# GpSimd's local attention products issued as two instructions, one for each head

## The chip, the cores and the metric

One NeuronCore of a Trainium2 chip runs the whole kernel. The metric is the device time of one execution in microseconds (us). Its compute engines, by the names of the profile, are PE (TensorE, matmuls), DVE (VectorE), ACT (ScalarE) and POOL (GpSimd); SP only issues DMAs.

## What is computed

Attention over q, k, v of shape (4, 8, 576, 64), then two pairs of dense layers on the 2304 rows of 512 that it leaves. The attention has two parts that are added: a downsampled one (mean over 4 tokens) and a local one, in which each token sees the seven tokens around it:

```python
mask = np.abs(pos[:, None] - pos[None, :]) < factor          # factor = 4
scores = np.where(mask, scale * np.matmul(q, k.transpose(0, 1, 3, 2)), -1e9)
attn = softmax(scores)
out = out_up + np.matmul(attn, v)
# then, on x = out as (2304, 512):
g = s * np.maximum(x @ w_in, 0) ** 2 + b;   x = g @ w_out
h = x @ w2_in;   out = (h - np.tanh(h)) @ w2_out
```

## The kernel before

The 2304 rows are cut into eight units of 288, u = 0 to 7. PE runs the first dense pair unit by unit (`l1`, line 741, into the tile `ph`; `l2_1`, line 774, into `acc`), each product as three matmuls on split operands (`gh` and `gl`, `wh` and `wl`). While PE works on unit u, the other engines make the attention of unit u + 1 (and begin that of u + 2), so that its x is there when PE comes to it. After unit 7 the second dense pair runs, with no attention beside it.

For units 2 to 7 the local attention is not made with matmuls. `local_items(u)` holds the two heads of a partition side by side (tiles `Q` of 128 x 2 heads x 9 tokens x 64, `K` and `V` with a window of 15 tokens) and makes, for each of NO = 7 offsets o, an elementwise product of 128 x 1152 elements:

- `mult(o, eng, kind)` makes Q times K (line 181), and `red(o)` sums it over the 64 elements into a score `s` (line 186, on DVE);
- after a softmax over the offsets (`sm1`, `sm2`), `pv(o, eng, kind)` makes V times the weight `a` (line 249), and `pvadd(o)` adds it to `O` (line 257, on DVE).

The constants `QK_POOL` and `PV_POOL` give two of the seven offsets in each part to POOL (tile `pP`); one or two of V times a go to ACT (`pA`), the rest to DVE (`pD`, `O`). So POOL makes 4 products in each of six units, 24 in all, and DVE reads each of them once. There is one buffer for each of `pP`, `pD` and `pA`: POOL's second product of a part waits until DVE has read the first. POOL also adds for the downsampled part (`raw`, line 350, and `pp`, line 351) and splits weights (`w`, line 730), and writes a column of ones into `gh` for unit 1 (line 761, a MEMSET).

`spread` puts the items of a unit into the 16 steps of the unit before by their costs (1.26 for an item of DVE, 0 for one of POOL), and a scheduler in the tile framework then orders the instructions of each engine by its own estimates, so an edit of one engine's instructions can move those of others. Each engine runs its own list in order.

Of the kernel before, what the change touches and what calls it, by code (L numbers as in the profile page):

```python
# [11 lines left out]
ALU = mybir.AluOpType  # L12
AX = mybir.AxisListType.X

B, H, S, D = 4, 8, 576, 64
# [8 lines left out]
SEG, TAU, WIN, NO = 18, 9, 15, 7  # L24
# [54 lines left out]
def attention_moe_moe_kernel(ctx: ExitStack, tc, q, k, v, w_in, w_out, s_in, b_in, w2_in, w2_out, out):  # L79
    nc = tc.nc  # L80
    pe, act, dve, pool, sp = nc.tensor, nc.scalar, nc.vector, nc.gpsimd, nc.sync
# [52 lines left out]
    Qt, Kt, Vt, Ot, X = {}, {}, {}, {}, {}  # L134
# [29 lines left out]
    def local_items(u):  # L164
# [4 lines left out]
        def ptile(shape, kind):  # L169
            t = {"O": "O", "p": "pP", "d": "pD", "a": "pA"}[kind]  # L170
            return late.tile(shape, F32, tag=t, name=t)
# [5 lines left out]
        def mult(o, eng, kind):  # L177
            def f():
                p = ptile([128, 2, TAU, D], kind)
                st[o] = p  # L180
                eng.tensor_tensor(out=p, in0=Qt[u], in1=Kt[u][:, :, o:o + TAU, :], op=ALU.mult)  # L181
            return f

        def red(o):
# [7 lines left out]
        d = [o for o in range(NO) if o not in qk_pool]  # L192
        p = list(qk_pool)
        busy, due = None, 0
        while d or p or busy is not None:
# [3 lines left out]
            elif d and due:  # L199
                o = d.pop(0)  # L200
# [6 lines left out]
            else:  # L207
                o = d.pop(0)
# [29 lines left out]
        def pv(o, eng, kind):  # L238
            def f():
                p_ = ptile([128, TAU, 2, D], kind)  # L240
                st["v", o] = p_
                if eng is act:
                    for h in range(2):
                        for t in range(TAU):
                            act.activation(out=p_[:, t, h], in_=Vt[u][:, h, o + t], func=AF.Copy,
                                           scale=st["a"][:, h * TAU + t, o:o + 1])
                    return
                aw = st["a"].rearrange("p (h t) o -> p t h o", h=2)[:, :, :, o:o + 1]
                eng.tensor_tensor(out=p_, in0=Vt[u][:, :, o:o + TAU, :].rearrange("p h t d -> p t h d"),  # L249
                                  in1=aw.to_broadcast([128, TAU, 2, D]), op=ALU.mult)  # L250
                if kind == "O":
                    Ot[u] = p_
            return f
# [6 lines left out]
        d = [o for o in range(NO) if o not in pv_pool and o not in pv_act]  # L260
# [658 lines left out]
    for s_, (n, u, i) in enumerate(seq):  # L919
# [10 lines left out]
        p_ = ps_ph.tile([128, NB1], F32, tag="ph", name="ph")  # L930
# [89 lines left out]
    for j in range(NBLK2):  # L1020
        for i in range(NF):
            p_ = ps_ph.tile([128, NB2], F32, tag="ph", name="ph2")
# [48 lines left out]
```

## Time and profile before

| | |
|---|---|
| time, median of 3 runs | 991.27 us |
| the three runs | 996.5, 991.27, 985.89 us |
| the profiled execution | 995.71 us, of which the span of the program 993.9 us |
| busy, share of the span | PE 950.1 us (96%), DVE 625.8 us (63%), ACT 473.3 us (48%), POOL 167.2 us (17%) |
| TensorE clock granted, mean | 0.961 of full speed |
| DMA | 80.85 MB, 81 GB/s on the mean |

All rows below are of that one profiled execution. A busy time counts what the profile takes as an instruction's duration, from its start to its end: an engine that has begun an instruction and is held up within it counts as busy. Idle time before an instruction stands in brackets behind a row, with what ended it. The engine that is busy 96% of the time can only be made to wait less; how much it waits is seen stage by stage.

### The profile page before, as it was taken

To read this page: it belongs to the slowest core of one execution; us is meant where nothing else is said; L and a number is where in the kernel's file an instruction comes from. 1 tells how busy PE (TensorE), PEld (TensorE's weight loads), DVE (VectorE), ACT (ScalarE), POOL (GpSimd) and SP (SyncE) were. 2 spreads that over 40 slices of the span, in tenths; PEclk is the share of its full clock that TensorE was granted. 3 is DMA by queue.
4 is the path that set the end of the run, shared out by engine and by line. 5 is a ranking of instruction groups with operands and counts; after the bars stand their busy time and mean duration, and the time that the engine had idled before them with its cause. 6 is when DMAs were issued, how large, how long until landed. Compare 5 with 4: busy or idle time off the path is not lost.

```text
span 993.9 us, 17097 instructions
## 1 busy us (share of the span) xinstructions
PE 950.1 (96%) x6554; PEld 879.4 (88%) x6554; DVE 625.8 (63%) x1102; ACT 473.3 (48%) x1352; POOL 167.2 (17%) x128
## 2 busy tenths in 40 slices
PE   8979998889989999999999999999999999999997
PEld 7868888779989989989999999999999999999996
DVE  4488898989999899796775962333333333333332
ACT  4549844436646564655586942332323232323222
POOL 1244453531613332241000000000000000000000
PEclk8559999979999999999999999999999999999999
DMA  9990053223222314120074810101001010100000
GB/s 226 303 347 1 3 198 112 77 78 130 76 83 98 96 49 134 30 64 1 25 276 179 291 46 1 43 2 43 22 22 41 3 43 1 44 1 22 1 22 21
DMA packets 59895, 80.85 MB, mean 81 GB/s; under 512 B 22454, under 2 KB 44710, under 8 KB 59814
## 3 DMA queue, kind: packets, MB, share of 16 engines
q1 hardware_dynamic: 59814, 79.76, 25.3%
q8 instruction: 51, 0.84, 0.3%
q14 instruction: 30, 0.25, 0.1%
HBM read 69.72 MB, written 10.03 MB: 80 GB/s over the span
## 4 chain that ended last, share of the span: by engine, by line
PE 57%; DVE 23%; issue 6%; DMA 6%; ACT 4%; POOL 2%; SPq 2%; DVEq 0%; POOLq 0%; ACTq 0%
PE ph L741 28%; PE acc L997 20%; PE acc L774 7%; DVE pp L353 3%; DVE O L257 3%; DVE s L186 2%; DVE pD L181 2%; DVE gl L762 2%; DVE wf L722 1%; DVE pD L249 1%; DMA K<-in_k_dram 1%; DMA wraw<-in_moe_w_in_dram 1%; DVE xq L314 1%; SPq L502 1%; DMA vraw<-in_v_dram 1%
## 5 line engine op out<-in xcount | busy, mean ns | idle before, releaser
L741 PE MATMUL ph<-xh,w 128*128 128x288 f32 x1024 | 238.3, 307 | 4.4 <-DVE gl L762 4.2
L774 PE MATMUL acc<-gh,w 128*128 128x288 f32 (+1 forms) x1024 | 230.5, 300 | 8.1 <-DVE yst L797 4.9
L741 PE MATMUL ph<-yxh,w 128*128 128x256 f32 x1152 | 228.4, 281 | 0.0
L741 PEld LDWEIGHTS ph<-yxh,w 128*128 128x128 f32 x1152 | 187.1, 189 | 6.3 <-DVE gl L985 0.2
L981 DVE TENSOR_TENSOR ph<-ph,th 128x256 f32<-128x256 f32 x144 | 62.3, 433 | 205.0 <-ACT th L980 204.9
L741 PEld LDWEIGHTS ph<-xh,w 128*128 128x128 f32 x1024 | 175.7, 193 | 11.9 <-DVE gl L762 7.3
L774 PEld LDWEIGHTS acc<-gh,w 128*128 128x128 f32 x1024 | 173.9, 191 | 11.0 <-DVE yst L797 5.9
L997 PE MATMUL acc<-w,gh 128*128 128x512 f32 x576 | 180.1, 393 | 0.0
L741 PE MATMUL ph<-yxl,w 128*128 128x256 f32 x576 | 161.9, 281 | 0.0
L741 PE MATMUL ph<-xl,w 128*128 128x288 f32 x512 | 154.7, 302 | 4.8 <-DVE xl L663 3.1
L980 ACT ACTIVATE th<-ph 128x256 f32<-128x256 f32 x144 | 55.5, 385 | 216.7 <-PE ph L741 216.7
L774 PE MATMUL acc<-gl,w 128*128 128x288 f32 x512 | 152.5, 298 | 0.3 <-DVE gl L762 0.3
L741 PEld LDWEIGHTS ph<-yxl,w 128*128 128x128 f32 x576 | 108.7, 189 | 6.2
L997 PE MATMUL acc<-w,gl 128*128 128x512 f32 x288 | 113.9, 395 | 0.0
L997 PEld LDWEIGHTS acc<-w,gh 128*128 128x128 f32 x576 | 98.6, 189 | 13.3
L741 PEld LDWEIGHTS ph<-xl,w 128*128 128x128 f32 x512 | 98.8, 193 | 6.3 <-DVE xl L663 3.5
L774 PEld LDWEIGHTS acc<-gl,w 128*128 128x128 f32 x512 | 97.6, 191 | 0.7 <-DVE gl L762 0.5
L985 DVE TENSOR_TENSOR gl<-ph,gh 128x256 fp32r<-128x256 f32 x144 | 61.0, 424 | 56.8 <-PE acc L997 29.9
L753 ACT ACTIVATE ph<-ph 128x288 f32<-128x288 f32 x128 | 51.3, 401 | 83.2 <-PE ph L741 80.6
L984 ACT CAST gh<-ph 128x256 fp32r<-128x256 f32 x144 | 53.8, 374 | 64.4 <-DVE ph L981 64.4
L762 DVE TENSOR_TENSOR gl<-ph,gh 128x288 fp32r<-128x288 f32 x128 | 57.4, 448 | 32.7 <-ACT gh L759 32.5
L997 PEld LDWEIGHTS acc<-w,gl 128*128 128x128 f32 x288 | 54.1, 188 | 12.4
(133 smaller groups left out, 1251.7 us busy)
## 6 DMA issues: line engine op xcount, KB each, us to landing
wraw<-in_moe_w_in_dram SPq DMA_DIRECT2D x32, 512.0 KB
wraw<-in_moe_w_out_dram SPq DMA_DIRECT2D x32, 512.0 KB
y<-yst SPq DMA_DIRECT2D x36, 144.0 KB
K<-in_k_dram SPq DMA_DIRECT2D x5, 960.0 KB
V<-in_v_dram SPq DMA_DIRECT2D x5, 960.0 KB
raw<-in_q_dram SPq DMA_DIRECT2D x24, 144.0 KB
raw<-in_k_dram SPq DMA_DIRECT2D x24, 144.0 KB
Q<-in_q_dram SPq DMA_DIRECT2D x6, 576.0 KB
```

Source lines behind the costliest of these rows:

```text
L181: eng.tensor_tensor(out=p, in0=Qt[u], in1=Kt[u][:, :, o:o + TAU, :], op=ALU.mult)
L257: dve.tensor_tensor(out=Ot[u], in0=Ot[u], in1=st["v", o], op=ALU.add)
L353: dve.tensor_reduce(out=t2.rearrange("p a h d -> p (a h) d").unsqueeze(3), in_=t[:GH].rearrange("p a h r d -> p (a h) d r"), axis=AX, op=A ...
L741: pe.matmul(p_, w_, x_, start=n == 0, stop=n == 3 * KC - 1)
L753: act.activation(out=p_, in_=p_, func=AF.Relu)
L762: dve.tensor_tensor(out=gl, in0=p_, in1=gh[:, :NB1].bitcast(F32), op=ALU.subtract)
L774: pe.matmul(accs[u][e][:, :g_.shape[1]], w_, g_, start=i == first and n == 0, stop=i == last and n == 2)
L980: act.activation(out=t, in_=p_, func=AF.Tanh)
L981: dve.tensor_tensor(out=p_, in0=p_, in1=t, op=ALU.subtract)
L984: act.copy(out=gh, in_=p_)
L985: dve.tensor_tensor(out=gl, in0=p_, in1=gh.bitcast(F32), op=ALU.subtract)
L997: pe.matmul(accs[j][t], g_, w_, start=i == 0 and n == 0, stop=i == NF - 1 and n == 2)
```

## The change

Where the engine is POOL, each of the two products is issued as two instructions, one for each head, over half of the same tiles. DVE and ACT keep theirs.

```diff
         def mult(o, eng, kind):
             def f():
                 p = ptile([128, 2, TAU, D], kind)
                 st[o] = p
-                eng.tensor_tensor(out=p, in0=Qt[u], in1=Kt[u][:, :, o:o + TAU, :], op=ALU.mult)
+
+                for h in ([slice(0, 1), slice(1, 2)] if eng is pool else [slice(0, 2)]):
+                    eng.tensor_tensor(out=p[:, h], in0=Qt[u][:, h], in1=Kt[u][:, h, o:o + TAU, :], op=ALU.mult)
             return f
...
-                eng.tensor_tensor(out=p_, in0=Vt[u][:, :, o:o + TAU, :].rearrange("p h t d -> p t h d"),
-                                  in1=aw.to_broadcast([128, TAU, 2, D]), op=ALU.mult)
+                vw = Vt[u][:, :, o:o + TAU, :].rearrange("p h t d -> p t h d")
+                aw = aw.to_broadcast([128, TAU, 2, D])
+                for h in ([slice(0, 1), slice(1, 2)] if eng is pool else [slice(0, 2)]):
+                    eng.tensor_tensor(out=p_[:, :, h], in0=vw[:, :, h], in1=aw[:, :, h], op=ALU.mult)
```

The change has four more lines than the kernel before, so its lines carry other numbers: 181 becomes 183, 186 becomes 188, 249 becomes 254, 257 becomes 261, 350 and 351 become 354 and 355, 761 becomes 765, 762 becomes 766 and 797 becomes 801.

In most of the 24 places POOL's list now has two rows where it had one, next to each other, and the second of them waits for nothing. Here is the list at the first product of unit 2, before and after (what an instruction waits for stands in brackets, as counters of engines and of DMA queues):

```order
L730 TENSOR_TENSOR w<-wf,w 128x512 [waits DMAHW6_49,Activation_49]
L761 MEMSET gh 128x2 [waits PE_49]
L181 TENSOR_TENSOR pP<-Q,K 128x1152 [waits DMAHW5_49,DMAHW4_49]
L761 MEMSET gh 128x2 [waits DVE_49,PE_49]
L181 TENSOR_TENSOR pP<-Q,K 128x1152 [waits DVE_49]
L350 TENSOR_TENSOR raw_1701<-raw_1701 72x4x128 [waits DMAHW2_49,DMAHW7_49,DMAHW1_49,DMAHW0_49]
```

And the same place of the change:

```order
L734 TENSOR_TENSOR w<-wf,w 128x512 [waits DMAHW6_49,Activation_49]
L765 MEMSET gh 128x2 [waits PE_49]
L183 TENSOR_TENSOR pP<-Q,K 128x576 [waits DMAHW5_49,DMAHW4_49]
L765 MEMSET gh 128x2 [waits DVE_49,PE_49]
L183 TENSOR_TENSOR pP<-Q,K 128x576
L183 TENSOR_TENSOR pP<-Q,K 128x576 [waits DVE_49]
L183 TENSOR_TENSOR pP<-Q,K 128x576
L354 TENSOR_TENSOR raw_1701<-raw_1701 72x4x128 [waits DMAHW2_49,DMAHW7_49,DMAHW1_49,DMAHW0_49]
```

The second product has become two rows in a row; of the first, the second half stands behind a MEMSET that waits for DVE and PE.

On DVE the scheduler has moved one instruction. This is DVE's list where PE has begun unit 5 and the last result of unit 4 is taken out of `acc` into `yst`; before:

```order
L353 TENSOR_REDUCE pp2_5188<-raw72_5090 72x256
L257 TENSOR_TENSOR O_5413<-O_5413,pA_5394 128x1152
L797 TENSOR_SCALAR yst_5041<-acc_4304,scal_86,bcol_87 128x288
L762 TENSOR_TENSOR gl_5068<-ph_5052,gh_5067 128x288
L257 TENSOR_TENSOR O_5413<-O_5413,pP_5535 128x1152
L181 TENSOR_TENSOR pD_5754<-Q_5322,K_5324 128x1152
L762 TENSOR_TENSOR gl_5114<-ph_5098,gh_5113 128x288
```

And the same place of the change:

```order
L357 TENSOR_REDUCE pp2_5206<-raw72_5107 72x256
L261 TENSOR_TENSOR O_5432<-O_5432,pA_5413 128x1152
L183 TENSOR_TENSOR pD_5775<-Q_5340,K_5342 128x1152
L801 TENSOR_SCALAR yst_5058<-acc_4317,scal_86,bcol_87 128x288
L766 TENSOR_TENSOR gl_5085<-ph_5069,gh_5084 128x288
L261 TENSOR_TENSOR O_5432<-O_5432,pP_5554 128x1152
L766 TENSOR_TENSOR gl_5131<-ph_5115,gh_5130 128x288
```

The product `pD` (of unit 7) has gone up by three rows, ahead of `yst`. On PE one group of three matmuls, on ACT one of the small `pA` instructions and on SP one store of y stand some rows elsewhere at the same place; everything else keeps its order.

## Rows read from the trace of the kernel before

**Rows 1.** Busy us (x instructions) of each engine by stretch, granted PE clock, DMA.

```profile
core 0: us, PE busy (x) PEld busy (x) DVE busy (x) ACT busy (x) POOL busy (x), PEclk, DMA share, GB/s
130.00:490.00 360.00, 333.16 (x2490) 315.98 (x2489) 324.55 (x456) 196.44 (x658) 118.62 (x64) 0.97 0.26 83
490.00:994.00 504.00, 497.57 (x3278) 458.12 (x3276) 208.80 (x457) 190.30 (x468) 0.00 (x0) 1.00 0.17 55
...
200.00:250.00 50.00, 43.68 (x313) 41.95 (x312) 45.60 (x71) 25.68 (x82) 11.52 (x6) 0.90 0.33 103
```

**Rows 2.** Chain of work that ended last: shares of the span by engine.

```profile
PE 57%; DVE 23%; issue 6%; DMA 6%; ACT 4%; POOL 2%; SPq 2%; DVEq 0%; POOLq 0%; ACTq 0%
```

**Rows 3.** Instructions by line: count, duration ns min/median/max, first and last start us.

```profile
L181 DVE TENSOR_TENSOR pD<-Q,K x30: 1324/1349/4227, 133.4 to 448.1; 128x1152 f32<-128x1152 f32 x30
L181 POOL TENSOR_TENSOR pP<-Q,K x12: 2609/2676/6080, 133.4 to 440.1; 128x1152 f32<-128x1152 f32 x12
...
L249 POOL TENSOR_TENSOR pP<-V,a x12: 2151/2720/3361, 172.1 to 479.6; 128x1152 f32<-128x1152 f32 x12
...
L730 POOL TENSOR_TENSOR w<-wf,w x24: 1266/1354/2158, 42.6 to 128.2; 128x512 fp32r<-128x512 f32 x24
```

**Rows 4.** DVE timeline, long instructions: start us, duration us, engine, line, operation, tiles.

```profile
139.32 3.30 DVE L181 TENSOR_TENSOR pD<-Q,K 128x1152 f32<-128x1152 f32 x1
...
173.29 3.31 DVE L249 TENSOR_TENSOR pD<-V,a 128x1152 f32<-128x1152 f32 x1
...
208.69 3.04 DVE L415 TENSOR_SCALAR E<-E,zz 72x144 f32<-72x144 f32 x4
...
269.75 2.27 DVE L410 TENSOR_SCALAR zz<-zz 72x4 f32<-72x4 f32 x1
...
430.24 4.23 DVE L181 TENSOR_TENSOR pD<-Q,K 128x1152 f32<-128x1152 f32 x1
...
480.26 2.68 DVE L257 TENSOR_TENSOR O<-O,pA 128x1152 f32<-128x1152 f32 x1
```

**Rows 5.** DVE timeline, instructions of the same kinds that were not held up.

```profile
193.75 0.48 DVE L415 TENSOR_SCALAR E<-E,zz 72x144 f32<-72x144 f32 x2
...
434.39 1.34 DVE L257 TENSOR_TENSOR O<-O,pA 128x1152 f32<-128x1152 f32 x1
...
436.03 0.15 DVE L410 TENSOR_SCALAR zz<-zz 72x4 f32<-72x4 f32 x1
```

**Rows 6.** POOL timeline, instructions back to back while DVE is held up.

```profile
50.68 2.49 POOL L730 TENSOR_TENSOR w<-wf,w 128x512 fp32r<-128x512 f32 x2
...
138.75 2.65 POOL L181 TENSOR_TENSOR pP<-Q,K 128x1152 f32<-128x1152 f32 x1 [1.43 <-DVE s L186]
141.37 2.40 POOL L350 TENSOR_TENSOR raw<-raw 72x512 f32<-72x512 f32 x1
...
429.33 1.30 POOL L350 TENSOR_TENSOR raw<-raw 72x512 f32<-72x512 f32 x1 [4.50 <-DMA y<-yst]
430.58 2.67 POOL L181 TENSOR_TENSOR pP<-Q,K 128x1152 f32<-128x1152 f32 x1
```

**Rows 7.** DVE timeline: one held up by POOL before 130 us, and one reduce.

```profile
50.39 3.33 DVE L722 SCALAR_TENSOR_TENSOR wf<-wraw 128x512 int32<-128x512 int32 x1
...
142.91 1.34 DVE L186 TENSOR_REDUCE s<-pD 128x18 f32<-128x1152 f32 x1
```

**Rows 8.** POOL's product and DVE's read of it, where DVE waits for it.

```profile
440.09 3.65 POOL L181 TENSOR_TENSOR pP<-Q,K 128x1152 f32<-128x1152 f32 x1 [6.36 <-DVE s L186]
...
443.78 1.35 DVE L186 TENSOR_REDUCE s<-pP 128x18 f32<-128x1152 f32 x1 [0.94 <-POOL pP L181]
```

**Rows 9.** PE timeline: three waits for DVE, with idle us and releaser.

```profile
211.27 0.30 PE L427 MATMUL PT<-ident,E 72*72 72x72 f32 x1 [4.59 <-DVE E L415]
...
424.79 0.40 PE L774 MATMUL acc<-gh,w 128*128 128x288 f32 x1 [1.03 <-DVE yst L797]
...
436.16 0.40 PE L741 MATMUL ph<-xh,w 128*128 128x288 f32 x1 [1.09 <-DVE gl L762]
```

## The prediction

> **What bounds the kernel now.** I read the busy time by stretch first. From 490 us on, PE is busy 497.57 of 504 us and POOL does nothing [rows 1]: no edit of POOL can shorten that half. The change acts from 130 to 490 us, where all of POOL's local products lie [rows 3]. There PE is busy 333.16 of 360 us and DVE 324.55, both about nine tenths: neither alone is the bound. PE works in order and waits, in short pieces, for DVE instructions that stand behind others in DVE's list [rows 9]. PE's idle time there, 360 - 333.16 = 26.8 us, is the most that faster work of DVE could give back, beside what the clock takes: it was granted at 0.97 of full speed on the mean there, and at 0.90 from 200 to 250 us. The chain of waits says the same in one line: PE 57%, DVE 23%, POOL 2% [rows 2]. POOL's own speed hardly matters; what it does to DVE does.
>
> It does something. A DVE product of 128 x 1152 takes 1.35 us on the median, but the longest 4.23 [rows 3]. The long ones stand in the timeline beside a POOL instruction: DVE's product at 139.32 took 3.30 us, and POOL's at 138.75 ended at 141.40, which is 1.2 us before DVE's end [rows 4, 6]. So DVE stood still until POOL was done, and then did its work. Ten DVE instructions between 130 and 490 us are held up by one of the 24 products, the first at 139.32 and the last at 480.26; six stand in rows 4 and their unhindered durations in rows 3 and 5. By each one's duration less the unhindered one, the ten lose 20.2 us together (1.95 at 139.32, 2.9 at 430.24, 1.3 at 480.26). Only DVE instructions with two inputs in SBUF are among them, and small TENSOR_SCALARs (zz, 2.27 us in place of 0.15); a reduce beside POOL keeps its 1.34 us [rows 4, 5, 7].
>
> **What the change does to this.** It removes no work: 24 POOL instructions become 48 of half the size.
>
> The price of a half: no half stands in the trace. The nearest row is POOL's 128x512 product, 1.27 us at least, against 2.61 for 128x1152 [rows 3]: 2.1 ns for each element and 0.19 us fixed, which makes 1.40 for 576 elements. Two back to back overlap by 0.05 us (2.49 for two of 1.27 [rows 6]), so a pair takes 2.75 us, 0.14 more than one. For V times a, 2.15 at least, I take the same 0.14. Bounds: nothing more at all, and twice the 0.19, that is 0.38. All 24 cost POOL 24 x 0.14 = 3.4 us, which its idle time hides: it is busy 118.62 of 360 us [rows 1].
>
> What matters is who goes next when the first half ends while DVE stands waiting. The trace shows both. At 141.40 POOL had its next instruction ready and DVE got in: POOL's sum `raw` took 2.40 us, waiting in its turn [rows 6]. But at 430.24 DVE waited while `raw` ran to 430.63, POOL's product followed at 430.58 and ran its plain 2.67 us, and DVE came after both, 4.23 us in all [rows 4, 6]. At 50.39 two equal products of POOL followed each other from 50.68 to 53.17 in 2.49 us, and DVE waited for both, 3.33 us in all [rows 6, 7]. That last case is the one nearest to two halves: same operation, same partitions, nothing to wait for in between. I take it: the pair stays glued, DVE waits as long as before and 0.14 more.
>
> The Trainium skill (SBUF — State Buffer, section "Who interferes with whom") says that whoever issues first "gets the shared pair for the whole instruction; the other fully blocks". The held-up rows above agree with it (3.30 against 1.35 us). Read to the letter it would let DVE in between two halves and speak for the change; that is the first rival below. The Trainium skill's GPSIMD Engine Reference (section "Instruction dispatch") says that POOL's cores start the next instruction as soon as each has finished its share of the one before, which speaks against it; the overlap of 0.05 us agrees.
>
> The sum if glued: 10 stalls x 0.14 = 1.4 us. Then DVE's reads of `pP` that already wait for POOL or come within 0.3 us of its end, like the one at 443.78 that idled 0.94 us [rows 8]: five, 5 x 0.14 = 0.7. Then the moved `pD`: `yst` now stands behind 1.35 us of it, and PE already waited 1.03 us for that `yst` at 424.79. PE starts 1.35 later there, but 11 us on it idled 1.09 us for DVE anyway, at 436.16 [rows 9], and DVE has no more to do than before; 0.3 is left (bounds 0 and 1.35). Behind the MEMSET that has come between the first product's halves stands POOL's second half and nothing urgent but DVE's read; the MEMSET had no idle time of its own before, so I take 0 (bound 1.4, if PE frees its buffer late). Sum +2.4 us, taking each us of DVE as one of the end, which is the upper price.
>
> The sum if DVE gets in every time: now what follows DVE's held-up instruction counts, since POOL's second half goes after it. A reduce or the short `gl`, in three of the ten, runs beside it: at 139.32, 173.29 and 269.75 DVE saves about half a product, 1.2 + 1.0 + 0.9 = 3.1 us. In the seven others the next instruction needs the same way in: at 430.24 an `O` sum follows [rows 5], and at 208.69 three more of the four TENSOR_SCALARs. It meets the second half, waits for the rest, and the 0.14 is lost: 7 x 0.14 = 1.0. Net -3.1 + 1.0 + 0.7 + 0.3 = -1.1 us. Either way it is at most a quarter of one per cent.
>
> The profiled execution took 995.71 us, 4.4 above the median of 991.27; the three runs lie 10.6 us apart. The forecast against its own time is 995.71 + 2.4 = 998.1, against the median 991.27 + 2.4 = 993.7. I forecast no change, at 993.7 us; its own range, from DVE let in every time (990.2) to the upper bounds of every term (10 + 5 times 0.38, 1.35, 1.4: +8.5), is 990 to 1000.
>
> **The rivals.**
>
> *Faster: every stall is halved.* If DVE gets in between the halves and keeps the way in for its next instruction too, ten stalls of 20.2 us become 10.1. Of this the end sees what PE waited for. The best case is at 211.27, where PE had idled 4.59 us for the `E` of rows 4 and the clock of that stretch was 0.90 [rows 1, 9]: at full clock all through, 50 x 0.10 = 5 us come back on top. 991.27 - 10.1 = 981.2, and 976 with the clock. For it: the handover at 141.40. Against it: the two cases at 50.39 and 430.24, and that seven of ten followers collide. It decides only if nearly all of the 10.1 us reach PE.
>
> *Slower: the read of `pP` comes late.* POOL now has to get in twice. If DVE lets each second half wait for one more of its products (1.35 us), POOL's result is 1.5 us late, and DVE, which reads it in the order of its list, idles; five products of the twelve of Q times K have less than that to spare (like the one in rows 8), 5 x 1.5 = 7.5 us, and with the moved `pD` (1.35) and the MEMSET (1.4) it is 10.3: 1001.5 us. A new fall of the clock to half speed would come on top. It decides once the five lose more than about 1.4 us each. Against it: between 441 and 444 us DVE runs a reduce, and this does not compete.
>
> *It does nothing at all that can be seen* is the forecast's own middle; it needs no other mechanism.
>
> **How the numbers follow.** About 1% is what a measurement of this kernel can tell from no change, since its runs lie that far apart. The forecast, glued or let in, has 0.74; the faster rival 0.13, the slower 0.13. Each rival ends at about 1% from 991.27, and the faster and slower chances are theirs: 0.13, 0.74, 0.13. The range goes from 984 (a good part of the faster rival's way, and the low runs of this kernel) to 1001 (the slower rival).
>
> **What would show it.** POOL's halves: 1.40 us alone for Q times K, about 1.15 for V times a, and 2.3 to 2.75 a pair. If glued, a DVE product that starts inside the first half ends 1.35 us after the end of the second, and POOL's two starts lie one plain half apart. If let in, DVE ends 1.35 us after the first half, and the second half is 1.35 us longer. DVE's excess over its plain durations: 20 to 22 us if glued, some 18 if let in with collisions, 10 if the rival is right. PE's wait before `yst` near 425 us: 2.3 us in place of 1.03, and none near 436. I would be wrong if a half cost far more than 1.4 us, if DVE idled for `pP` more than 3 us in all, or if the granted clock from 200 to 250 us rose or fell with it.

## The result, and the profile after

| | before | change |
|---|---|---|
| time, median of 21 runs each | 991.27 us | 1002.21 us |
| lowest and highest run | 979.46, 998.88 us | 990.14, 1009.41 us |
| the profiled execution, span | 993.9 us | 997.7 us |
| TensorE clock granted, mean of it | 0.961 | 0.964 |

The change is slower: ratio 1.0127, 95% interval 1.0094 to 1.0159. The forecast of 993.7 us is missed, and so is its range of 984 to 1001, by 1.2 us at its upper end. A second measurement of the same kernel (e5, below) gave a ratio of 1.0054 [1.0008, 1.0099], so the size is less certain than the sign. Every ratio here is taken over the faster group of each kernel's runs (within 1.5% of its fastest), so it is not the quotient of the medians, which are over all runs.

The single spans cannot be compared as they stand. How long the clock is at half speed in the first 75 us differs by execution, in code that the change does not touch: in the twelve traces of this study PE begins unit 0 anywhere from 53.6 to 67.5 us. Two measures avoid this, and both are used below.

- **Units 2 to 7½ in the trace.** PE issues 96 matmuls of `ph` (line 741 before, 745 after) in each half of a unit, so the start of each 96th dates PE's progress. From the first matmul of unit 2 to the middle of unit 7 it took 326.1 us before and 333.1 us in the change: +7.0. This leaves out unit 1, beside which the products for unit 2 run: its first half took 39.53 us before and 43.05 in the change, its second 45.70 and 41.26. With unit 1 taken in, the change took 6.1 us longer.
- **Equal clock.** Over the 77 runs of the kernel before, 0.01 of mean granted clock goes with 7.5 us of span (a straight line fits with 1.6 us left over). These 77 are the runs measured beside e1 to e10; the change's 21 runs, for which no chip is on record, lie 6.5 ± 0.4 us above their line. A fall of the clock that a new wait brings about is taken out by this measure.

Both say 6 to 7 us. From unit 2 on, two halves of units have all of it: 3.0 to 3.5 (the first half of unit 3) took 30.86 us before and 34.83 in the change, 5.0 to 5.5 took 32.05 and 35.98. The others together are 0.9 us shorter.

The rows that answer to [rows 1] (busy us of PE, PEld, DVE, ACT and POOL with instructions, clock, DMA share, GB/s):

```profile
130.00:490.00 360.00, 326.25 (x2443) 309.81 (x2443) 313.73 (x454) 190.69 (x639) 136.54 (x88) 0.97 0.25 79
490.00:994.00 504.00, 501.44 (x3309) 462.22 (x3307) 210.02 (x458) 194.13 (x483) 0.00 (x0) 1.00 0.17 55
```

DVE lost 10.8 us of busy time at nearly the same number of instructions (456 and 454), POOL gained 17.9. PE did 47 matmuls fewer in the same 360 us and had them left for later. By line, as in [rows 3]:

```profile
L183 DVE TENSOR_TENSOR pD<-Q,K x30: 1328/1348/2059, 131.3 to 450.9; 128x1152 f32<-128x1152 f32 x30
L183 POOL TENSOR_TENSOR pP<-Q,K x24: 1396/1428/4825, 131.2 to 445.2; 128x576 f32<-128x576 f32 x24
...
L254 POOL TENSOR_TENSOR pP<-V,a x24: 1157/1726/4658, 172.1 to 484.9; 128x576 f32<-128x576 f32 x24
L254 DVE TENSOR_TENSOR pD<-V,a x13: 1341/1357/2326, 173.3 to 479.3; 128x1152 f32<-128x1152 f32 x13
```

DVE's longest product of Q and K fell from 4.23 to 2.06 us. POOL's halves run 1.40 and 1.16 us alone, but the longest 4.83. So DVE is let in between the halves wherever it stood waiting, and now POOL waits. DVE's product of [rows 4] at 173.29 (3.31 us) and POOL's pair beside it, in the change:

```profile
173.32 2.32 DVE L254 TENSOR_TENSOR pD<-V,a 128x1152 f32<-128x1152 f32 x1
```

```profile
172.09 4.58 POOL L254 TENSOR_TENSOR pP<-V,a 128x576 f32<-128x576 f32 x2 [4.58 <-DVE a L236]
```

DVE gets its 1.0 us back; POOL's pair takes 4.58 us where one product took 3.32. Over all 24, POOL's products went from 71.4 us (38.6 and 32.8) to 90.0 (44.0 and 46.0): what DVE no longer stands still, POOL does.

Where that reaches PE is told by the chain of work that ended last, from 420 to 432 us of the change (start us, us, what):

```profile
420.57 1.17 POOL pP L254
421.74 4.79 POOL pp L355
426.54 0.02 issue
426.55 0.32 SPq L346
426.87 0.05 issue
426.92 0.02 SPq L803
426.94 0.04 issue
426.98 2.39 DMA y<-yst
429.37 0.03 issue
429.40 0.05 DVEq L801
429.44 0.05 issue
429.49 0.58 DVE yst L801
430.08 0.04 issue
430.12 2.05 PE acc L778 x7
```

It reads: POOL's first half ends; the sum `pp` (line 355), which stands between the halves, takes 4.79 us; with it a buffer of `raw` comes free, so SP can issue its load `raw` <- v (line 346); behind that load in SP's list stands a store of y (line 803); the store frees one of the two buffers of `yst`; DVE fills it out of `acc` (line 801); and PE, which needs that `acc`, goes on. DVE had `pD` behind it by 425.94 and then stood idle for that store:

```profile
424.59 1.35 DVE L183 TENSOR_TENSOR pD<-Q,K 128x1152 f32<-128x1152 f32 x1
429.49 0.57 DVE L801 TENSOR_SCALAR yst<-acc,scal,bcol 128x288 f32<-128x288 f32 x1 [3.55 <-DMA y<-yst]
```

PE's own rows say how long it stood there, [rows 9] having 1.03 at 424.79 and 1.09 at 436.16:

```profile
302.49 0.40 PE L778 MATMUL acc<-gh,w 128*128 128x288 f32 x1 [3.36 <-DVE yst L801]
...
430.12 0.61 PE L778 MATMUL acc<-gh,w 128*128 128x288 f32 x1 [4.68 <-DVE yst L801]
```

Near 302 us the wait was 0.91 before. After both waits the granted clock fell for a while to the lower of its two levels (1.2 GHz), so a stretch of 9 us around each had 0.81 on the mean; e9 (below), without these waits, had 1.00 in both stretches:

```profile
299.00:308.00 9.00, 5.64 (x32) 4.98 (x32) 6.54 (x10) 2.17 (x11) 2.67 (x2) 0.81 0.38 117
425.00:434.00 9.00, 4.32 (x23) 3.62 (x22) 3.73 (x6) 4.46 (x18) 5.67 (x4) 0.81 0.27 83
```

### The profile page after: what moved, and what is told of

Read it like the earlier page. It is cut to its first block, busy times and chain, and to the rows that moved or that the text cites. A ratio compares the mean times of both kernels' runs of the same rounds, so it can differ in the third digit from the quotient of the medians.

```text
span 997.7 us, 17122 instructions
## 1 busy us (share of the span) xinstructions
PE 946.9 (95%) x6554; PEld 878.0 (88%) x6554; DVE 618.3 (62%) x1102; ACT 472.8 (47%) x1352; POOL 185.1 (19%) x152
## 4 chain that ended last, share of the span: by engine, by line
PE 48%; DVE 10%; issue 7%; POOL 3%; ACT 2%; DMA 2%; POOLq 0%; SPq 0%; DVEq 0%; ACTq 0%
PE ph L745 24%; PE acc L1001 20%; PE acc L778 4%; DVE s L188 2%; POOL pP L254 1%; DVE gl L766 1%; DVE pD L183 1%; DVE O L261 1%; DVE pp L357 1%; ACT pA L247 1%; POOL pp L355 1%; DMA wraw<-in_moe_w_out_dram 1%; DMA y<-yst 1%; POOL pP L183 1%; DVE xq L318 1%
## 5 line engine op out<-in xcount | busy, mean ns | idle before, releaser
L254 POOL TENSOR_TENSOR pP<-V,a 128x576 f32<-128x576 f32 x24 | 46.0, 1936 | 109.9 <-DVE O L261 63.4
```

The source lines that it names most:

```text
L254: eng.tensor_tensor(out=p_[:, :, h], in0=vw[:, :, h], in1=aw[:, :, h], op=ALU.mult)
```

## The experiments

Three theories stood against each other. QUEUE: POOL's late work holds up SP's load, and with it the store of y, `yst` and PE, as in the chain above. ORDER: what costs is the moved order of the other engines (`pD` ahead of `yst` on DVE and what goes with it), not POOL's pace. SPREAD: the loss is in small pieces over all the pairs, as late reads of `pP`. Each ratio is against runs of the kernel before from the same measurement. The next three columns are of one trace each (PE's longest wait for `yst` near 425 us, the half-unit that holds it, units 2 to 7½, in us); the last is the us above the line at equal clock, over all runs, with its standard error.

| kernel | median us (runs) | ratio [95%] | PE wait | 5.0-5.5 | 2-7½ | equal clock |
|---|---|---|---|---|---|---|
| before | 991.27 (21) | | 1.03 | 32.05 | 326.1 | 0 |
| change | 1002.21 (21) | 1.0127 [1.0094, 1.0159] | 4.68 | 35.98 | 333.1 | +6.5 ± 0.4 |
| e5 change again | 998.0 (12) | 1.0054 [1.0008, 1.0099] | 5.22 | 36.17 | 333.1 | +6.9 ± 0.5 |
| e1 one pair whole | 997.69 (6) | 1.0115 [1.0053, 1.0178] | 1.45 | 32.30 | 329.1 | +4.6 ± 0.6 |
| e2 two pairs whole | 994.07 (12) | 1.0054 [1.0004, 1.0105] | 1.00 | 32.27 | 328.1 | +4.1 ± 0.5 |
| e3 only Q times K | 996.4 (12) | 1.0107 [1.0058, 1.0156] | 1.41 | 32.22 | 326.0 | +2.8 ± 0.4 |
| e4 only V times a | 999.76 (6) | 1.0135 [1.0074, 1.0196] | 4.74 | 35.21 | 333.7 | +4.9 ± 0.6 |
| e6 halves adjacent | 996.52 (12) | 1.0007 [0.9951, 1.0062] | 1.13 | 32.52 | 329.5 | +5.1 ± 0.4 |
| e9 `yst` first | 995.81 (10) | 1.0044 [0.9985, 1.0103] | 1.42 | 31.36 | 326.6 | +3.1 ± 0.5 |
| e7 change, 4 `yst` | 997.24 (12) | 1.0038 [0.9986, 1.0091] | none | 33.03 | 329.8 | 0.0 ± 0.6 |
| e8 before, 4 `yst` | 992.03 (12) | 0.9968 [0.9911, 1.0024] | none | 29.47 | 326.1 | -1.8 ± 0.4 |
| e10 e6, 4 `yst` | 995.85 (10) | 0.9996 [0.9951, 1.0041] | none | 32.39 | 329.0 | +0.2 ± 0.4 |

Ratios of one kernel differ by as much between measurements as most of these differ from each other (e5 and the change are one kernel). The runs of the kernel before on the three chips of e1 to e10 lie -0.9 to +0.4 us about their common line; -0.9 is the chip of e9 and e10, so against its own runs of the kernel before they lie 4.0 and 1.1 us above, not 3.1 and 0.2. So what follows rests on the waits in the traces first, and on the last column second.

**e5: the change once more.** No edit.

> The change itself, once more, for a second trace and for its time beside the next three. QUEUE: PE waits 4 to 5 us for yst near 425 us again, DVE 3 to 4 us for y's store before it; the wait of 3.4 us near 299 us need not come again, since it was not in the trace with one product whole, where the same rows stood. From the start of unit 2 to the middle of unit 7 it takes 330 to 334 us (326.1 before, 333.1 in the change's first trace).

The trace repeats: the waits of 3.33 and 5.22 us at the same two places (the second a little over the 4 to 5 expected), 34.78 and 36.17 us in the same two half-units, 333.1 us over units 2 to 7½; with unit 1 taken in, 7.1 us more than before. The loss has fixed places; it is not an accident of one execution.

**e1 and e2: one and two of the V times a pairs whole again.** The product at (unit 6, offset 6) is the one near 421 us; e2 also takes (4, 4), near 290 us.

```diff
-                for h in ([slice(0, 1), slice(1, 2)] if eng is pool else [slice(0, 2)]):
+                for h in ([slice(0, 1), slice(1, 2)] if eng is pool and (u, o) not in ((6, 6),) else [slice(0, 2)]):
```

> The change, but the one product whose halves have a pp sum between them (the second V times a of unit 6, near 420 us) is one instruction again; on PE, DVE, ACT and SP every row then stands as in the kernel before. Three theories of the 11 us (1.3%) that the change costs. QUEUE: the halves make POOL's pp sums late at two places (near 299 and 425 us), SP's load of raw waits for the sum, the store of y behind it waits, DVE's yst finds no free buffer and PE waits for yst; it says that PE's wait near 425 us falls from 4.7 us to about 1, the one near 299 us stays at 3.4, and 3.5 to 6 us come back (about 996 to 998.5 against 1002). SPREAD: POOL and DVE collide more in all 24 places alike; it says 1/24 comes back, 1001.5. ORDER: only the moved rows cost; it says that all comes back, 991.

> As the run before, and the first V times a of unit 4 (near 289 us) is one instruction too; 22 products stay split. QUEUE: both waits are gone, 991 to 995. SPREAD: 2/24 comes back, 1001. ORDER: the same as with one, 991.

With one product of 24 whole, the order of every other engine returns to that of before, and PE's wait near 425 us is 1.45 in place of 4.68. That one place is 3.7 us of the 7 in the trace (35.98 to 32.30); at equal clock 1.9 us came back. Both times lie where QUEUE expected them. It does not say whether POOL or the moved order was at fault, since both went back together. The wait near 302 us, which was expected to stay in e1, went there too, with nothing done to it (0.88 us): that place is decided by something finer (below, the sum and the reduce).

**e3 and e4: the two kinds of product apart.** e3 splits only Q times K (line 183), e4 only V times a (line 254).

> Only the 12 products Q times K are split; every row of PE, DVE, ACT and SP stands as before. QUEUE: both late sums come from V times a, so 990 to 994, and the two waits of PE for yst near 300 and 425 us stay at about 1 us. SPREAD: half of the loss, 996.5. ORDER: 991.

> Only the 12 products V times a are split; the rows of the other engines stand as in the change. QUEUE: the whole loss, 1000 to 1004, with PE's waits of 3 to 5 us near 300 and 425 us. SPREAD: half of it, 996.5. ORDER: the whole loss, 1002, all of it near 425 us.

In e4 the wait near 425 us is there (4.74 us) and the one near 302 us, which QUEUE expected too, is not (0.96). In e3 neither is, and its trace takes 326.0 us over units 2 to 7½, as before. So the loss at these places belongs to the V times a pairs. Over the whole it is the larger part of it: with unit 1 taken in, e4's trace is 3.4 us longer than before and e3's 1.5, at equal clock they lie 4.9 and 2.8 us above the line. e3's time missed QUEUE's 990 to 994; 996.4 is what SPREAD said. Its runs had a mean granted clock of 0.959, and on its ratio of 1.0107 alone the case is inconclusive. Where Q times K costs is seen in the faster rival below.

**e6: all pairs split, the halves adjacent.** The second half at (6, 6) is given a higher priority in the scheduler, so that POOL's sum stands behind both halves. The order of the other engines is then as before.

```diff
-                    eng.tensor_tensor(out=p_[:, :, h], in0=vw[:, :, h], in1=aw[:, :, h], op=ALU.mult)
+                    with ahead(3000 if (u, o) == (6, 6) else 0):
+                        eng.tensor_tensor(out=p_[:, :, h], in0=vw[:, :, h], in1=aw[:, :, h], op=ALU.mult)
```

> The change with all 24 products split, but the second half of the one at 425 us has a higher priority for the scheduler, so that POOL's pp sum stands behind both halves and not between them; PE, DVE, ACT and SP have the rows of the kernel before. QUEUE: PE's wait near 425 us falls to 1 to 1.5 us, unit 2 to 7 takes 329 us, the time 3 to 6 us below the change's. If it is the split product itself that costs there and not the place of the sum, the wait stays over 3 us.

PE's wait is 1.13 us with all 24 products in halves: what cost 3.9 us near 425 us was where the sum and the other rows came to stand, not the split as such. The runs show less of it than the trace: at equal clock e6 lies 1.8 us below e5, the change on the same chip, and its median 1.5, where 3 to 6 were expected.

**e9: all pairs split, POOL's list as in the change, `yst` ahead.** This keeps the sum between the halves. It puts `yst` back on DVE, lets SP issue both stores before the load, and with that the rows that had moved on PE and ACT go back too.

```diff
-                dve.tensor_scalar(out=t, in0=a_, scalar1=scal[:, 0:1], scalar2=bcol[:, e:e + 1],
-                                  op0=ALU.mult, op1=ALU.add)
+                with ahead(200 if (u, e) == (4, 1) else 0): dve.tensor_scalar(out=t, in0=a_, scalar1=scal[:, 0:1],
+                                  scalar2=bcol[:, e:e + 1], op0=ALU.mult, op1=ALU.add)
```

> The change with all 24 products split, and with POOL's list just as in the change (the sum pp, line 355, still stands between the two halves of the second V times a product near 421 us). One thing is taken back: the second yst of unit 4 on DVE (line 801) is put ahead of pD and gl, and with it SP's list issues two stores of y (line 803) before the two loads raw <- in_v (line 346), where the change has one store, a load, a store, a load. QUEUE theory (what is paid near 425 us is a store of y that stands on SP behind a load which waits for POOL's late sum): POOL's sum stays late (about 4 us or more, ending past 425.5), but no yst of DVE waits over 1 us for a store there, PE's wait near 425 us falls from 4.7 to 1.0 to 1.5 us, and the half-unit 5.0 to 5.5 takes about 32.3 us, as where the pair is whole or the halves are adjacent; time 993 to 998 us. POOL theory (the late sum itself is paid, through the load behind it and the products that need it, wherever the store stands): the half-unit stays at 35 to 36 us. The place near 299 us is not touched; it goes by the phase of that execution.

POOL and SP of e9 (near 412 us, since unit 0 began 8 us earlier there), then SP of the change and of the kernel before at the same place:

```profile
410.79 1.17 POOL L254 TENSOR_TENSOR pP<-V,a 128x576 f32<-128x576 f32 x1 [18.89 <-DVE O L261]
411.92 3.46 POOL L355 TENSOR_TENSOR pp<-raw 72x256 f32<-72x256 f32 x1
415.34 1.17 POOL L254 TENSOR_TENSOR pP<-V,a 128x576 f32<-128x576 f32 x1
```

```profile
409.02 2.54 SPq L803 DMA_DIRECT2D y<-yst  x2
415.40 0.76 SPq L346 DMA_DIRECT2D raw<-in_v_dram  x2
```

```profile
419.06 0.38 SPq L803 DMA_DIRECT2D y<-yst  x1
426.55 0.32 SPq L346 DMA_DIRECT2D raw<-in_v_dram  x1
426.98 0.35 SPq L803 DMA_DIRECT2D y<-yst  x1
```

```profile
418.59 2.76 SPq L799 DMA_DIRECT2D y<-yst  x2
424.86 0.33 SPq L342 DMA_DIRECT2D raw<-in_v_dram  x1
```

The sum is still late (3.46 us, where it takes 0.73 undisturbed and took 2.50 here in the kernel before), and the load still waits for it (415.40). But two stores of y are out before that load, and PE waits 1.42 us:

```profile
415.33 0.40 PE L778 MATMUL acc<-gh,w 128*128 128x288 f32 x1 [1.42 <-DVE yst L801]
```

In the change the second store stands behind the load and goes at 426.98. So a late sum alone costs PE next to nothing here (0.4 us of waiting more than before); with the store queued behind its load it costs 3.9 us. QUEUE is shown for this place, and ORDER is half right. That the row that counts in the moved order is SP's is read from the chain (DVE idles 3.55 us for the store) and not from e9 alone, which put all the moved rows back. `pD` adds to it by making POOL's sum wait for one product more (4.82 us, where e9's took 3.46). e9's trace takes 326.6 us over units 2 to 7½, half a us from before, with every product split, and its median of 995.81 us lies where QUEUE expected it.

Near 302 us no row of SP has moved: there the store stands behind the load in the kernel before too, where the sum ended at 296.97:

```profile
297.00 0.30 SPq L342 DMA_DIRECT2D raw<-in_v_dram  x1
297.34 0.38 SPq L799 DMA_DIRECT2D y<-yst  x1
```

In the change these two go at 298.80 and 299.15, once the sum has ended. So at that place ORDER has nothing to say: the wait of 3.36 us comes with the late sum and with no moved row.

**e7, e8 and e10: four buffers of `yst`.** If the way to PE is the wait for a `yst` buffer, more of them close it at both places.

```diff
-YB = 2
+YB = 4
```

> The change with four buffers for yst in place of two, so that taking a unit out of acc waits for no store of y (some rows of all engines move with it). QUEUE: no wait of DVE for y's store and of PE for yst over 2 us is left; unit 2 to 7 takes within 2 us of what the kernel before takes with the same four buffers. SPREAD (POOL and DVE colliding in all places): 5 us or more above it.

> The kernel before with four buffers for yst: the control of the run above. Its waits for y's store were 0.2 to 1.9 us on ACT and none on DVE, so QUEUE expects it 0 to 3 us faster than the kernel before, 988 to 997 us, and if so the fastest of all.

> The change with the halves adjacent at the second V times a product of unit 6 (as in e6) and with four buffers of yst in place of two (as in e7 and e8). QUEUE theory: both ways by which POOL's lateness reached PE are closed, so what is left of the change is the spread part alone (late reads of pP, the longer wait of PE near 150 us): 1 to 4 us more than before with four buffers (992.0), 993 to 996 us, and units 2.0 to 7.5 in 327 to 330 us. If instead four buffers only shift the wait, as e7's new waits for gl and E near 330 and 436 us suggest, it lands at e7's 997 and 330 to 331 us. In either case it does not beat the kernel before.

No DVE or ACT instruction waits over 1 us for a store in e7 or e8, and at equal clock the change now lies 1.8 us above its counterpart (0.0 against -1.8) in place of 6.5. So some 4 to 5 us did come by way of `yst`. The rest moved rather than went: e7's trace still takes 3.7 us more than e8's (329.8 and 326.1), over the 2 that QUEUE allowed, with new waits such as

```profile
439.25 0.40 PE L745 MATMUL ph<-xh,w 128*128 128x288 f32 x1 [3.00 <-DVE gl L766]
```

and e10, with both remedies, has 2.37 us there and 329.0, inside the 327 to 330 expected from QUEUE. No ratio of the kernels tried is below 1 by more than its interval; e8's 0.9968 [0.9911, 1.0024] includes 1, though at equal clock it lies 1.8 us below the line.

## Why the prediction failed, step by step

**The price of a half: right.** Forecast 1.40 and about 1.15 us alone, 2.3 to 2.75 a pair. Measured 1.40 and 1.16 at least, pairs of 2.80 (at 197.07 us) and 2.30 (at 190.04).

**"The pair stays glued": wrong.** DVE is let in between the halves wherever it stood waiting. The excess of DVE's products held up by POOL's went from 20.2 to about 11 us: this is what the rival *faster* said of the stalls (10.1). The case chosen as nearest, [rows 7] at 50.39, is in the trace of the change too, and DVE still takes 3.3 us there, where 0.69 is its median: it stands through the end of one POOL instruction and the two equal ones after it.

```profile
47.97 0.72 POOL L528 TENSOR_TENSOR vd<-vraw 72x256 f32<-72x256 f32 x1
48.65 2.48 POOL L734 TENSOR_TENSOR w<-wf,w 128x512 fp32r<-128x512 f32 x2
```

```profile
48.37 3.32 DVE L726 SCALAR_TENSOR_TENSOR wf<-wraw 128x512 int32<-128x512 int32 x1
```

Why those two products of POOL shut DVE out and two halves never do was not tried and stays open. The Trainium skill's page SBUF — State Buffer (section "Who interferes with whom") has the lock held "for the whole instruction"; the 2.32 us at 173.32 agree with a handover at each instruction's end, the 3.32 us at 48.37 do not.

**"POOL's own speed hardly matters; what it does to DVE does": the step that lost the case.** It was read off POOL's 2% in the chain [rows 2] and its idle time [rows 1], and so the sum priced POOL at 0.14 us a pair, 3.4 us in all, hidden. POOL became 17.9 us busier, because the standing still passed from DVE to POOL, and in three places work that PE needs stands behind POOL: not the products, but the sum `pp`, behind it on SP a load, and in two of them, near 302 and 425 us, a store. PE's two waits for `yst` were 3.36 and 4.68 us, where 0.91 and 1.03 had stood. The share of an engine on the chain says what bounds now, not what it can lose. The rival *slower* asked the right question, what is late when POOL has to get in twice, but followed only the reads of `pP`. Those went from 2.5 to 5.9 us of DVE's idle time. That is past the 3 us named as a sign of being wrong, but the rise stays below the 7.5 that the rival priced, and none of PE's long waits ends on one of them.

**The moved `pD`: mis-sized, 0.3 us for 3.9.** Forecast was a wait of 2.3 us near 425 and none near 436. None came near 436, but the wait was 4.68: the price counted DVE's 1.35 us and left out the row that moved on SP, though the lists of the change showed it. It is this store that e9 puts back.

**The MEMSET between the halves: 0, right.** PE never waits for its `gh`; PE's longest idle time there, for `yst`, was 1.17 us before and 1.13 after.

**The faster rival: its stalls came true, its time did not.** PE's wait for `E` at 211.27 [rows 9], where it saw the best case, became 5.10 and 0.62 us. Even so the half-unit that holds it fell from 45.70 to 41.26 us; in all seven traces with unit 2's V times a in halves and two `yst` it is 40.98 to 43.08, in e3 45.40. Near 148 us, where DVE was let in and got ahead, it then waited for a load that came no sooner:

```profile
148.06 1.94 DVE L357 TENSOR_REDUCE pp<-raw 72x256 f32<-72x1024 f32 x1 [2.70 <-DMA raw<-in_k_dram]
```

That load stands behind a late sum `pp` as well: DVE being ahead, the sum now begins within DVE's reduce and takes 2.81 us, the load goes at 144.88, and PE waits for DVE. The change, then e4, where Q times K is whole:

```profile
142.04 2.81 POOL L355 TENSOR_TENSOR pp<-raw 72x256 f32<-72x256 f32 x1
```

```profile
150.05 0.42 PE L379 MATMUL qkps<-ident,pp 72*128 72x72 f32 x2 [3.30 <-DVE pp L357]
```

```profile
142.61 0.74 POOL L355 TENSOR_TENSOR pp<-raw 72x256 f32<-72x256 f32 x1
```

```profile
149.20 0.34 PE L379 MATMUL qkps<-ident,pp 72*128 72x72 f32 x2 [1.02 <-DVE pp L357]
```

In all seven traces with Q times K in halves and two `yst` the wait is 3.26 to 3.57 us and the first half of unit 1 takes 41.27 to 44.26; in the kernel before and e4 it is 1.01 and 1.02 us, 39.53 and 38.19. So the halves of Q times K cost here, and in unit 1 what V times a gives back hides it.

**What stays open.** The wait near 302 us is the other 4 us of the traced loss from unit 2 on. The chain there is the same (the sum ends at 298.77, the load goes at 298.80, the store at 299.15), and with four `yst` it is gone; but no experiment undid that place alone, and in every trace but the change's and e5's it did not come up. And e9 is 3.1 us above the line at equal clock (4.0 above its own chip's runs) where its trace shows 0.5: whether other executions of it lose more near 302 us, or the pairs cost a little everywhere, the runs do not tell.

## What to carry to other kernels

Before an engine with idle time is given more pieces to do, follow what stands *behind* those pieces in its list, and from there through every queue: a buffer that comes free late, the load that waits for it, and whatever was queued behind that load. When a scheduler moves rows, price the rows of the DMA queue as well as those of the engines; here one store moved behind one load was 3.9 us of the traced 7, though undoing it gave back only 1.8 to 3.4 us at equal clock. And letting a waiting engine in sooner moves the wait to the other engine: it is a gain only if that one has nothing urgent next.

## What the runs showed of the hardware

POOL's sum `pp` (72 x 256) takes 0.73 us, but not when it begins while DVE is in its reduce of `raw` (72 x 1024, 2.0 us). In the twelve traces 37 of these sums began in that reduce, and all 37 ended after it; at 0.73 us, 25 of them would have ended within it. They ended 0.3 to 0.9 us after it in seven cases, where DVE's next instruction was a `gl`; 1.86 in most, where a product of 128 x 1152 followed at once; 3.12 where two did; and 4.0 in the three traces with four `yst`, near 299 us, there too behind a `gl`. It looks as if POOL stood through the reduce and then through DVE's products too. The change's twelve sums by line (ns min/median/max), and POOL and DVE near 295 us:

```profile
L355 POOL TENSOR_TENSOR pp<-raw x12: 724/1432/4822, 142.0 to 448.4; 72x256 f32<-72x256 f32 x12
```

```profile
294.96 3.81 POOL L355 TENSOR_TENSOR pp<-raw 72x256 f32<-72x256 f32 x1
```

```profile
294.89 2.02 DVE L357 TENSOR_REDUCE pp<-raw 72x256 f32<-72x1024 f32 x1
296.83 1.34 DVE L261 TENSOR_TENSOR O<-O,pD 128x1152 f32<-128x1152 f32 x1
```

And e9 at the same place, where POOL's sum began 0.08 us before the reduce in place of 0.07 us after it:

```profile
287.26 0.74 POOL L355 TENSOR_TENSOR pp<-raw 72x256 f32<-72x256 f32 x1
```

```profile
287.34 2.02 DVE L357 TENSOR_REDUCE pp<-raw 72x256 f32<-72x1024 f32 x1 [0.22 <-DMA raw<-in_k_dram]
```

Of the nine traces with two `yst`, only those of the change and e5 have this sum begin in the reduce, and only they have the wait near 302 us. Which of the two begins first does not settle it everywhere: in e7 a sum begun 0.05 us before that reduce took 3.94 us. It is no general rule of reduces either: the same sum beside a reduce of `s` (128 x 1152, 1.35 us) takes 0.73, and a first half of V times a begun in the same reduce of `raw` took its plain 1.17 us (251.96, in the reduce at 251.80). What sets this sum apart was not tried.
